# Attention weights in 20 blocks for 26: the low halves of P packed backwards before the transposing DMAs, with a new order of the work

## The chip, the cores and the metric

The kernel runs on one core of one Trainium2 chip. Its engines are named as in the profile: PE (TensorE, the matmuls; PEld its weight loads), DVE (VectorE), ACT (ScalarE), POOL (GpSimd) and SP (SyncE, whose queue issues the DMAs). The metric is the device time of one execution in microseconds: 638.75 us before, the median of 3 runs (637.15 to 640.37).

## What is computed

Causal softmax attention over 4 batches of 12 heads, 448 rows and 64 columns, followed by a two-layer network with squared relu; all inputs and outputs are float32.

```python
def reference(q, k, v, w_in, w_out):          # q, k, v: (4, 12, 448, 64)
    scores = q @ k.transpose(0, 1, 3, 2) / 8  # 64 ** -0.5
    scores = where(upper triangle, -1e9, scores)
    p = exp(scores - max); p = p / (sum(p) + 1e-9)
    o = p @ v
    x = o.transpose(0, 2, 1, 3).reshape(1792, 768)
    g = maximum(x @ w_in, 0) ** 2             # w_in (768, 2048)
    return g @ w_out                          # w_out (2048, 768)
```

## The kernel before

**Halves.** Float32 operands of the large matmuls are split into a float16 high half and a float16 remainder, the low half. A product is three float16 matmuls: high by high, high by low, low by high. High halves are made on ACT, DVE or POOL (`hi`, L479 and L487), low halves nearly all on DVE (`lo`, L492).

**Attention.** A head's 448 rows are cut into NCH = 4 chunks of P = 112, so its causal P (the softmax weights) has NB10 = 10 blocks of 112x112 that are not empty. Heads are worked on in pairs (NPAIR = 6 for each batch). For one head of a pair the steps are: scores on PE (L751, into a PSUM bank); mask and row maximum on DVE (L734); exponential on ACT (L738) into `pq`; reciprocal row sums on DVE (L774, L777); `halves`, which writes P's high and low half into `psrc` and then issues one transposing DMA `pt<-psrc` on SP (L665); P times V on PE, `values16` (L791, 24 matmuls of a pair), from `pt`; a copy of the result as high half (L803 on ACT or L804 on DVE) and low half (L807, DVE) into `xt`, which is x transposed. In batches 2 and 3 q and k are split too and turned by transposing DMAs (`qk<-qs`, L689).

**The slots of `psrc`.** Chunk c of the rows holds c + 1 blocks, kc = 0 to c. In half z of a whole pair the block (c, kc) is written to slot `z * 13 + c + 3 * kc`: 13 slots (NSL) for 10 blocks, so that for one kc the blocks of all c lie side by side and one matmul of `values16` takes them together. Three slots of each half are empty; they are zeroed once by `pads` (L1561 to L1566), as is the 16-column strip behind each block. Batch 1 goes through in two parts: the first (chunks 0 and 1) has 3 slots for each half, the second (chunks 2 and 3) 8 for 7 blocks. The DMA turns all slots, so 26, 16 or 6 blocks.

**The network.** First layer: for each 128 columns of the hidden layer 18 matmuls (L1239) on 256 or 128 columns of x, relu (L1202) and square (L1209) on ACT or DVE, and halves of g. Second layer: 24 matmuls in a PSUM bank (L1257), then an eviction on ACT (L1269) for the first half of the sum or on DVE (L1274) for the second, then `out_dram<-ob`. The weights `wi` and `wo` are loaded and split in the first part of the program. The V of a batch needs a common scale: `vnorm` loads all of it in six pieces `vn` (L544, one buffer) and sums its squares on ACT (L546).

**Stages.** Batch 0's attention is done in float32 form (early parts, L644 its normalisation) while weights arrive; then batch 0's network beside the attention of batch 1; the network of each further batch beside the attention of the next; at the end `products_block` does the first layer of batch 3 by seven half-size products in place of eight (L1461 its matmuls, L1469 their sums). Its weight sums are made on DVE (L1346) and stored in the areas of `qk`, `qs`, `pt`, `psrc` and `pq`, so they begin when the attention of batch 3 is through with these.

**What sets the order.** Every operation is recorded in a `Plan` with its engines, a cost in ns, the tiles it reads and writes and a due time. The due time is made from a table of numbers, `PR` (a base and a rate for each stage, an offset for each kind of operation, a bias for each choice of engine). `Plan.order` is a list scheduler: it goes through model time and gives each free engine the ready operation with the earliest due time; for an operation that two engines can do it also picks the engine. The result is one fixed list for each engine, and the engines run their lists strictly in order. SP's list holds all DMAs.

Of the kernel before, what the change touches and what calls it, by code (L numbers as in the profile page):

```python
# [1625 lines left out]
```

## Time and profile before

| | |
|---|---|
| median of 3 runs | 638.75 us |
| the profiled execution | 639.5 us |
| its span (first to last record) | 637.8 us |
| PE busy | 601.7 us, 94% |
| DVE busy | 508.4 us, 80% |
| ACT busy | 460.5 us, 72% |
| POOL busy | 32.0 us, 5% |
| mean granted PE clock | 0.997 of full speed |

The times are microseconds from the span's start. A row of the timeline gives start, duration, engine, line of the kernel, operation, tiles (out<-in) and count; in square brackets stands how long the engine had been idle before, and what released it. The list of waits adds up such idle times by the line that waited and the line waited for. A row "PE bank L791 <- DMA pt<-psrc" says that a matmul of L791 on PE waited for a transposing DMA. The windows show busy time of each engine in a stretch, with the share of full speed that the clock of PE was granted.

### The profile page before, as it was taken

What the parts mean: (1) busy time and instruction counts of PE and PEld (TensorE: products, weight loads), DVE (VectorE), ACT (ScalarE), POOL (GpSimd) and SP (SyncE); (2) the same over time, 40 slices, a digit from 0 to 9 for tenths busy, and PEclk for the clock granted to TensorE, in tenths of its full rate; (3) what the DMA queues carried; (4) which work ended last, traced back from release to release, by engine and by line L of the source; (5) the groups of instructions that cost most, each with busy time, mean ns of one, the idle gap of its engine ahead of it and who ended that gap; (6) DMA issues with size and microseconds to landing.
All of it is one profiled execution on the core that took longest, in us unless ns stands there. A gap on an engine that the chain in (4) does not pass through costs nothing.

```text
span 637.8 us, 14221 instructions
## 1 busy us (share of the span) xinstructions
PE 601.7 (94%) x5178; PEld 442.0 (69%) x5178; DVE 508.4 (80%) x1535; ACT 460.5 (72%) x1332; POOL 32.0 (5%) x45
## 2 busy tenths in 40 slices
PE   6888998979999989999999999999999999899997
PEld 4555687769665567877667767887768776687664
DVE  3899999999887899888879949768898999975100
ACT  4898898968797779877889849989847266485000
POOL 0000000001100000000000222323000000000000
PEclk9999999999999999999999999999999999999999
DMA  9974565564756877858999799994840000000100
GB/s 215 336 225 144 167 228 177 192 202 148 170 115 152 199 158 164 176 107 179 201 205 176 149 206 181 195 179 96 168 107 15 13 12 13 2 1 13 39 26 25
DMA packets 209158, 87.33 MB, mean 137 GB/s; under 512 B 196544, under 2 KB 203968, under 8 KB 209088
## 3 DMA queue, kind: packets, MB, share of 16 engines
...
q8 instruction: 40, 0.66, 0.4%
...
## 4 chain that ended last, share of the span: by engine, by line
PE 53%; DVE 21%; DMA 11%; ACT 10%; issue 2%; SPq 1%; ACTq 0%; DVEq 0%
PE bank L1257 23%; PE bank L1239 15%; DMA pt<-psrc 6%; PE bank L1461 5%; PE bank L791 3%; DVE pq L1346 3%; DMA vn<-in_v_dram 3%; PE bank L751 3%; DVE wi L996 2%; DVE wi L993 2%; ACT pq L738 1%; ACT psrc L479 1%; DVE bank L881 1%; DVE psrc L492 1%; DVE bank L734 1%
## 5 line engine op out<-in xcount | busy, mean ns | idle before, releaser
L1257 PE MATMUL bank<-wo,g 128*128 128x384 f16 x1056 | 183.9, 327 | 2.0 <-ACT ob L1269 1.3
L1239 PE MATMUL bank<-xt,wi 128*128 128x256 f16 (+1 forms) x1728 | 169.8, 256 | 2.9 <-ACT r L1202 2.6
L1239 PEld LDWEIGHTS <-wi 128*128 128x128 f16 x1728 | 145.0, 98 | 20.8 <-issue 5.5
L1257 PEld LDWEIGHTS <-g 128*128 128x128 f16 x1056 | 101.7, 98 | 67.0 <-issue 6.1
L492 DVE SCALAR_TENSOR_TENSOR psrc<-pq,nm,psrc 112x112 f16<-112x112 f32 (+3 forms) x144 | 71.8, 526 | 6.5 <-ACT psrc L479 6.0
L479 ACT ACTIVATE psrc<-pq,nm 112x112 f16<-112x112 f32 (+3 forms) x144 | 66.7, 525 | 11.1 <-DMA pt<-psrc 5.3
L738 ACT ACTIVATE pq<-bank,nm 112x224 f32<-112x224 f32 (+3 forms) x144 | 69.5, 490 | 7.3 <-DVE nm L734 6.3
L1269 ACT ACTIVATE ob<-bank,fac 128x384 f32<-128x384 f32 x26 | 15.1, 579 | 55.4 <-PE bank L1257 50.0
L1274 DVE SCALAR_TENSOR_TENSOR ob<-bank,fac,ob 128x384 f32<-128x384 f32 x26 | 16.0, 614 | 47.3 <-PE bank L1257 47.2
L734 DVE CUSTOM_DVE_ANT_0 bank<-bank,mask,sc 112x112 f32<-112x112 f32 (+3 forms) x96 | 46.8, 512 | 6.8 <-PE bank L751 6.4
L487 DVE TENSOR_TENSOR g<-g,g 128x256 f16<-128x256 f32 (+1 forms) x96 | 38.1, 410 | 10.3 <-ACT g L479 10.1
L1209 ACT ACTIVATE g<-r 128x256 f32<-128x256 f32 (+1 forms) x96 | 34.9, 376 | 7.4 <-DVE g L487 2.9
L479 ACT ACTIVATE g<-g 128x256 f16<-128x256 f32 (+1 forms) x96 | 35.4, 392 | 0.5
L751 PE MATMUL bank<-qk 128*112 128x336 f16 (+3 forms) x192 | 32.4, 285 | 2.0 <-ACT pq L738 1.2
L791 PE MATMUL bank<-pt,vp 112*64 112x224 f16 (+3 forms) x504 | 31.5, 268 | 1.1 <-DMA pt<-psrc 1.1
L791 PEld LDWEIGHTS <-vp 112*64 112x64 f16 x504 | 23.7, 109 | 12.4 <-issue 8.9
L1461 PEld LDWEIGHTS <-wi 128*128 128x128 f16 x288 | 28.2, 98 | 5.8 <-issue 2.1
L738 ACT ACTIVATION_READ_ACCUMULATOR pq<-bank,nm 112x1 f32 x144 | 29.0, 202 | 0.0
L751 PEld LDWEIGHTS <-qk 128*112 128x112 f16 x192 | 21.4, 130 | 7.9 <-issue 2.4
L1202 ACT ACTIVATE r<-bank 128x256 f32<-128x256 f32 (+1 forms) x64 | 20.2, 324 | 7.5 <-PE bank L1239 7.3
L873 PE MATMUL bank<-wo 64*96 64x256 f32 (+4 forms) x144 | 19.8, 387 | 6.0 <-ACT wo L650 3.5
L881 DVE CUSTOM_DVE_ANT_0 bank<-bank,mask 128x128 f32<-128x128 f32 (+3 forms) x48 | 21.4, 492 | 4.2 <-PE bank L873 3.9
...
## 6 DMA issues: line engine op xcount, KB each, us to landing
...
```

The lines of the kernel that those rows point to most:

```text
L479: nc.scalar.activation(out=o, in_=i, func=ACTF.Copy, scale=s)
L487: return plan.add({"dve": dve_ns(n), "pool": pool2_ns(n)}, lambda e: engines[e].tensor_tensor(out=out(), in0=in_(), in1=top(), op=ALU.subt ...
L492: nc.vector.scalar_tensor_tensor(out=out(), in0=in_(), scalar=scale(), in1=top(), op0=ALU.mult, op1=ALU.subtract)
L734: one("dve", dve_ns(w, 1, 2 if F16S[b] else 1) - 10, lambda e: nc.vector.tensor_tensor_reduce(out=s.ap[0:P, 0:w], in0=s.ap[0:P, 0:w], in1= ...
L738: one("act", act_ns(w, True, 1, True), lambda e: nc.scalar.activation(out=p32[j].ap[0:P, b0 * P:b0 * P + w], in_=s.ap[0:P, 0:w], func=ACTF ...
L751: nc.tensor.matmul(out=s.ap[0:P, 0:(c + 1) * P], lhsT=qT.ap[:, j * NCH + c, :], rhs=kT.ap[:, a:a + c + 1, :].rearrange("p a t -> p (a t)") ...
L791: nc.tensor.matmul(out=pv.ap[j * D:(j + 1) * D, ca * P:t1], lhsT=vp.ap[:, hv, vb:vb + D], rhs=pT[j].ap[0:P, hp * ns + x:hp * ns + x + w, : ...
L881: one("dve", dve_ns(w, 1, 1) - 10, lambda e, c=c, j=j, w=w, ss=ss, nm=nm: nc.vector.tensor_tensor_reduce(out=ss[j].ap[0:M, 0:w], in0=ss[j] ...
L1209: nc.scalar.activation(out=g32.ap[:, 0:n], in_=r.ap[:, 0:n], func=ACTF.Square)
L1239: nc.tensor.matmul(out=h.ap[:, 0:n], lhsT=wi_hl(ci, hw)[:, ms], rhs=x[:, kd, hx, off:off + n], start=(kd == 0 and hw == 0 and hx == 0), st ...
L1257: nc.tensor.matmul(out=o.ap[:, 0:HALF], lhsT=gsl(kf, hg, tt * 128, (tt + 1) * 128), rhs=wo_hl(kf, hw)[:, hh * HALF:(hh + 1) * HALF], start ...
L1461: nc.tensor.matmul(out=ps.ap[:, 0:n], lhsT=A[0](f, kd, hw)[:, ms], rhs=B[0](kd, hx), start=(kd == 0 and hw == 0 and hx == 0), stop=(kd == ...
```

## The change

The high half keeps its slots `c + 3 * kc`. The low half of a whole pair is no longer written 13 slots further on, but backwards from LOW = 16: block (c, kc) goes to slot `16 + c - 4 * kc`. The two halves together fill slots 0 to 19, the low half's blocks standing partly in the gaps of the high half, and 20 slots are turned instead of 26. For one kc the blocks of all c still lie side by side, so `values16` has as many matmuls as before and only starts at other slots. The second part of batch 1 uses step -2 from -3, 7 slots for each half, so 14 blocks instead of 16; its first part stays at 6. No slot is empty any more, and `pads` zeroes only the strips behind the blocks, in one instruction for each tile instead of four. The planner's costs of these DMAs and of the pads are set to smaller numbers, and the table `PR` holds new numbers throughout.

```python
half(z): slots at, at + by, ..., at + by * c      # c + 1 blocks of chunk c
  z = 0:              at = c - first,  by = step (3)
  z = 1, whole pair:  at = 16 + c,     by = -4
```

```diff
--- before.py
+++ after.py
@@ -19,57 +19,56 @@
 PR = {
-    "B1": -4922121, "B2": -1256835, "B3": -7452496, "E0": -10267855, "ER": -76227, "F0": -3309169, "FR": 520466,
...
+    "B1": -4911717, "B2": -688992, "B3": -6548886, "E0": -11820246, "ER": 45535, "F0": -3500830, "FR": 591205,
...
@@ -653,20 +652,28 @@
 
     def halves(due, cs, src, skey, rr, rkey, ps, pT, pj):
         first, step, ns = SLOTS[cs[0], len(cs)]
+        n2 = 2 * (NB10 if ns == NSL else ns)
         a = 0
         for c in cs:
             w = (c + 1) * P
-            half = lambda z, c=c: ps.ap[0:P, z * ns + c - first:z * ns + c - first + step * c + 1:step, 0:P]
+            def half(z, c=c):
+                at, by = z * ns + c - first, step
+                if z and ns == NSL:
+                    at, by = LOW + c, -4
+                end = at + by * c
+                return ps.ap[0:P, at:at + 1 if c == 0 else end + 1 if by > 0 else end - 1 if end else None:by if c else 1, 0:P]
+
             from_ = lambda a=a, c=c: src()[:, a:a + c + 1, :]
             a += c + 1
             hi(w, lambda half=half: half(0), from_, lambda c=c: rr(c, c + 1), [(skey, c), rkey], [(ps, c, 0)], due)
             lo(w, lambda half=half: half(1), from_, lambda c=c: rr(c, c + 1), lambda half=half: half(0),
                [(skey, c), rkey, (ps, c, 0)], [(ps, c, 1)], due, [(skey, c)])
-        one("sp", {3: 870.0, 8: 2180.0}.get(ns, 3135.0), lambda e: nc.sync.dma_start_transpose(
-            out=pT.ap[:, 0:2 * ns], in_=ps.ap[0:P, 0:2 * ns].rearrange("p a d -> p (a d)")),
-            [(ps, c, z) for c in cs for z in range(2)] + [("pads", pj)], [pT], due, {3: 1320.0, 8: 1770.0}.get(ns, 3430.0), extra=150.0)
-
-    SLOTS = {(0, NCH): (0, NCH - 1, NSL), (0, 2): (0, 1, 3), (2, 2): (2, 2, 8)}
+        one("sp", {3: 870.0, 7: 1910.0}.get(ns, 2420.0), lambda e: nc.sync.dma_start_transpose(
+            out=pT.ap[:, 0:n2], in_=ps.ap[0:P, 0:n2].rearrange("p a d -> p (a d)")),
+            [(ps, c, z) for c in cs for z in range(2)] + [("pads", pj)], [pT], due, {3: 1320.0, 7: 1600.0}.get(ns, 2650.0), extra=150.0)
+
+    LOW = 16
+    SLOTS = {(0, NCH): (0, NCH - 1, NSL), (0, 2): (0, 1, 3), (2, 2): (-3, -2, 7)}
 
     def pair(i, sc=None, cs=tuple(range(NCH))):
         b, pr = divmod(i, NPAIR)
@@ -784,8 +791,11 @@
         def values16(e):
             for kc in range(c1):
                 ca = max(kc, c0)
-                x, w = step * kc + ca - first, c1 - ca
+                w = c1 - ca
                 for z, (hv, hp) in enumerate(((0, 0), (0, 1), (1, 0))):
+                    x = step * kc + ca - first
+                    if hp and ns == NSL:
+                        x = LOW + ca - 4 * kc - ns
                     for j in range(2):
                         vb = (j * c1 + kc if c1 == NCH else 2 * kc + j) * D
                         nc.tensor.matmul(
@@ -1558,7 +1568,7 @@
             out=minus, in_=minus, pattern=[[-1, 128]], compare_op=ALU.is_equal, fill=0.0, base=0, channel_multiplier=1)
 
     def pads(e, t):
-        for w in (t[:, :, P:], t[:, 6:15:8, 0:P], t[:, 20:21, 0:P], t[:, 23:25, 0:P]):
+        for w in (t[:, 0:2 * NB10, P:],):
             if e == "act":
                 nc.scalar.activation(out=w, in_=mask[0:P, 0:w.shape[2]].unsqueeze(1).to_broadcast(list(w.shape)), func=ACTF.Copy)
             else:
@@ -1573,7 +1583,7 @@
     pos, last1 = sub_block(0, 256, 128, 256, [(128, 0)], pos, "n", True)
     last1(last0(pos))
     for j in range(2):
-        plan.add({"dve": 900, "act": 1250}, lambda e, t=psrc[j][0:P]: pads(e, t), [], [n_ps(j), ("pads", j)], ("a", H, "ld"), "pad", True)
+        plan.add({"dve": 400, "act": 360}, lambda e, t=psrc[j][0:P]: pads(e, t), [], [n_ps(j), ("pads", j)], ("a", H, "ld"), "pad", True)
     attention(1)
     pos = 0.0
     for b in range(1, B):
```

Line numbers after the change: 1 less up to the function `halves`, 6 more for its DMA (L665 is L671), 10 more from `values16`'s matmul on (L791 is L801, L1239 is L1249, L1257 is L1267).

The new numbers in `PR` move instructions on every engine. PE has the same matmuls in both. Seven L644 move from DVE to ACT (L642), six 448-column copies from ACT (L803) to DVE (L804), six pad instructions of ACT fall away. On PE, the last matmul of L791 stands at row 6815 of 9281 before and at row 6755 after; of the second-layer matmuls (L1257), those between it and the last 312 of them are 234 before and 264 after. Before, 66 of them stand in a row ahead of the last products; now 24 and 48, with one product (9 matmuls) between.

ACT, in the front, where the network of batch 0 goes from blocks of 256 columns to one of 128; before:

```order
L1202 ACTIVATE r<-bank_119 128x256
L1209 ACTIVATE g_1705<-r 128x256
L479 ACTIVATE g<-g_1705 128x256
L546 ACTIVATE junk,vst<-vn 128x448
L479 ACTIVATE wo<-wo,wst 128x768
L1202 ACTIVATE r<-bank_119 128x128
L1202 ACTIVATE r<-bank_123 128x128
```

and after:

```order
L1212 ACTIVATE r<-bank_119 128x256
L1219 ACTIVATE g_1681<-r 128x256
L478 ACTIVATE g<-g_1681 128x256
L478 ACTIVATE wo<-wo,wst 128x768
L545 ACTIVATE junk,vst<-vn 128x448
L1212 ACTIVATE r<-bank_119 128x128
L478 ACTIVATE wo<-wo,wst 128x768
```

The split of a piece of `wo` has moved ahead of the square of a piece of V (`junk,vst<-vn`), and only one of the two relus on 128 columns stands directly behind. On PE, between the last 256-column matmuls of the first layer and the first 128-column ones, there are now 6 small matmuls of L1082 and 6 of the second layer; before, the two followed each other.

SP, in the attention of batch 1, from a 6-block transpose of its first part on; before:

```order
L665 DMA_TRANSPOSE pt<-psrc_145 128x6x112
L614 DMA raw<-in_q_dram 112x4x64
L614 DMA raw<-in_k_dram 112x4x64
L544 DMA vn<-in_v_dram 128x448
L665 DMA_TRANSPOSE pt<-psrc_146 128x6x112
L665 DMA_TRANSPOSE pt<-psrc_145 128x6x112
L665 DMA_TRANSPOSE pt<-psrc_146 128x6x112
L614 DMA raw<-in_q_dram 112x4x64
L603 DMA raw<-in_k_dram 112x4x64 x2
L614 DMA raw<-in_q_dram 112x4x64
L665 DMA_TRANSPOSE pt<-psrc_145 128x6x112
L665 DMA_TRANSPOSE pt<-psrc_146 128x6x112
```

and after:

```order
L671 DMA_TRANSPOSE pt<-psrc_145 128x6x112
L543 DMA vn<-in_v_dram 128x448
L671 DMA_TRANSPOSE pt<-psrc_146 128x6x112
L671 DMA_TRANSPOSE pt<-psrc_145 128x6x112
L1288 DMA out_dram<-ob 128x384
L671 DMA_TRANSPOSE pt<-psrc_146 128x6x112
L543 DMA vn<-in_v_dram 128x448
L1288 DMA out_dram<-ob 128x384
L613 DMA raw<-in_q_dram 112x4x64
L602 DMA raw<-in_k_dram 112x4x64
L543 DMA vn<-in_v_dram 128x448
L671 DMA_TRANSPOSE pt<-psrc_145 128x6x112
```

Loads `vn` of batch 1's V (L544, now L543) and two outputs (`out_dram<-ob`, L1278, now L1288) have come among the transposes. Behind the first `pt<-psrc` there is one load `vn` before and seven after; on ACT, four squares stand behind the first exponential (L738) of this stage before and seven after.

DVE, where attention ends and the weight sums of the last block begin; before:

```order
L774 TENSOR_SCALAR nm<-sm 112x4
L777 RECIPROCAL nm<-nm 112x4
L492 SCALAR_TENSOR_TENSOR psrc_146<-pq,nm,psrc_146 112x112
L492 SCALAR_TENSOR_TENSOR psrc_146<-pq,nm,psrc_146 112x2x112
L492 SCALAR_TENSOR_TENSOR psrc_146<-pq,nm,psrc_146 112x3x112
L807 SCALAR_TENSOR_TENSOR xt_143<-bank_103,xt_143 128x448
L492 SCALAR_TENSOR_TENSOR psrc_146<-pq,nm,psrc_146 112x4x112
L1346 TENSOR_TENSOR pq<-wi 128x512 x3
L1346 TENSOR_TENSOR pq<-pq 128x512
L1274 SCALAR_TENSOR_TENSOR ob<-bank_131,fac,ob 128x384
```

and after:

```order
L781 TENSOR_SCALAR nm<-sm 112x4
L1284 SCALAR_TENSOR_TENSOR ob<-bank_131,fac,ob 128x384
L784 RECIPROCAL nm<-nm 112x4
L491 SCALAR_TENSOR_TENSOR psrc_146<-pq,nm,psrc_146 112x112
L491 SCALAR_TENSOR_TENSOR psrc_146<-pq,nm,psrc_146 112x2x112
L814 TENSOR_SCALAR xt_143<-bank_103 128x448
L491 SCALAR_TENSOR_TENSOR psrc_146<-pq,nm,psrc_146 112x3x112
L817 SCALAR_TENSOR_TENSOR xt_143<-bank_103,xt_143 128x448
L491 SCALAR_TENSOR_TENSOR psrc_146<-pq,nm,psrc_146 112x4x112
L1356 TENSOR_TENSOR pq<-wi 128x512 x3
L1356 TENSOR_TENSOR pq<-pq 128x512
```

The copy `xt_143<-bank_103` (ACT's L803 before) is DVE's L814 here, between two low halves, and an eviction into `ob` stands ahead of the reciprocal instead of behind the first sums.

## Rows read from the trace of the kernel before

**Rows 1.** The page's span and part 1: busy time, share, instructions by engine.

```profile
span 637.8 us, 14221 instructions
...
PE 601.7 (94%) x5178; PEld 442.0 (69%) x5178; DVE 508.4 (80%) x1535; ACT 460.5 (72%) x1332; POOL 32.0 (5%) x45
```

**Rows 2.** Windows: busy us (count) PE, PEld, DVE, ACT, POOL; clock, DMA, GB/s.

```profile
280.00:480.00 200.00, 196.61 (x1678) 145.63 (x1676) 164.52 (x542) 162.79 (x485) 26.75 (x30) 1.00 0.82 164
480.00:560.00 80.00, 76.33 (x684) 59.11 (x683) 76.41 (x187) 45.17 (x126) 0.00 (x0) 1.00 0.03 9
```

**Rows 3.** Waits of PE, 480 to 640 us: us in total, times, longest.

```profile
PE bank L1461 <- DVE pq L1469: 2.3, 3, 1.1
PE bank L1257 <- ACT ob L1269: 1.3, 2, 0.7
PE bank L1257 <- DVE ob L1274: 0.7, 1, 0.7
```

**Rows 4.** Waits of PE, 160 to 480 us.

```profile
PE bank L765 <- ACT raw L650: 2.4, 4, 1.3
PE bank L751 <- ACT pq L738: 1.2, 2, 1.0
PE bank L791 <- DMA pt<-psrc: 1.1, 3, 0.7
```

**Rows 5.** Timeline of PE, 135 us on: start, duration, work, count, [idle, releaser].

```profile
139.68 3.16 PE L1239 MATMUL bank<-xt,wi 128*128 128x128 f16 x36 [2.18 <-ACT r L1202]
```

**Rows 6.** Windows, 464 to 474 us: columns as in Rows 2.

```profile
464.00:474.00 10.00, 9.71 (x67) 5.79 (x66) 9.95 (x19) 4.09 (x8) 0.00 (x0) 1.00 0.72 170
```

**Rows 7.** L665 and L492, 280 to 480 us: ns min/median/max, first, last start.

```profile
L665 SPq DMA_TRANSPOSE pt<-psrc x24: 3016/3270/5123, 291.7 to 466.8; - x24
...
DMA to landing us min/median/max: 4.7/5.4/7.4
...
L492 DVE SCALAR_TENSOR_TENSOR psrc<-pq,nm,psrc x96: 322/556/1457, 284.8 to 464.7; 112x112 f16<-112x112 f32 x24, 112x224 f16<-112x224 f32 x24, 112x336 f16<-112x336 f32 x24, 112x448 f16<-112x448 f32 x24
```

**Rows 8.** Timeline of ACT from 135 us.

```profile
137.97 0.58 ACT L546 ACTIVATE junk<-vn 128x448 bf16<-128x448 f32 x1 [1.79 <-DMA vn<-in_v_dram]
...
138.54 0.92 ACT L479 ACTIVATE wo<-wo,wst 128x768 f16<-128x768 f32 x1
```

**Rows 9.** The chain that ended last: start, duration, work, count.

```profile
486.63 3.90 PE bank L1257 x24
```

**Rows 10.** Windows, 138 to 144 us: columns as in Rows 2.

```profile
138.00:140.00 2.00, 0.32 (x6) 0.32 (x6) 1.00 (x3) 2.00 (x7) 0.00 (x0) 1.00 0.19 28
140.00:142.00 2.00, 2.00 (x29) 2.00 (x26) 2.00 (x5) 2.00 (x6) 0.00 (x0) 0.66 0.24 87
142.00:144.00 2.00, 2.00 (x13) 1.32 (x12) 2.00 (x4) 1.54 (x7) 0.00 (x0) 0.50 0.66 135
```

**Rows 11.** Waits of ACT, 85 to 160 us.

```profile
ACT junk L546 <- DMA vn<-in_v_dram: 5.9, 4, 1.8
```

**Rows 12.** Timeline of PE, 547 to 554 us.

```profile
547.37 1.14 PE L1461 MATMUL bank<-raw,wi 128*128 128x256 f16 x9 [1.06 <-DVE pq L1469]
...
550.17 0.49 PE L1461 MATMUL bank<-raw,qs 128*128 128x256 f16 x3 [0.68 <-DVE pq L1469]
...
553.88 2.12 PE L1461 MATMUL bank<-raw,wi 128*128 128x256 f16 x18 [0.60 <-DVE pq L1469]
```

**Rows 13.** Lines L644, L803 and L1563: ns min/median/max.

```profile
L644 DVE TENSOR_SCALAR psrc<-psrc,nm x6: 393/432/454, 65.7 to 118.0; 96x448 f32<-96x448 f32 x3, 96x352 f32<-96x352 f32 x3
...
L803 ACT ACTIVATE xt<-bank x18: 333/526/544, 192.8 to 474.7; 128x448 f16<-128x448 f32 x12, 128x224 f16<-128x224 f32 x6
...
L1563 ACT ACTIVATE psrc<-mask x8: 312/412/577, 122.6 to 126.7; 112x224 f16<-112x224 bf16 x4, 112x416 f16<-112x416 bf16 x2, 112x112 f16<-112x112 bf16 x2
```

**Rows 14.** Timeline of ACT, 160 to 170 us.

```profile
160.89 0.58 ACT L546 ACTIVATE junk<-vn 128x448 bf16<-128x448 f32 x1 [0.53 <-DMA vn<-in_v_dram]
...
168.60 0.58 ACT L546 ACTIVATE junk<-vn 128x448 bf16<-128x448 f32 x1 [0.58 <-DMA vn<-in_v_dram]
```

More of the change, by code (lines that the diff above doesn't have):

```diff
@@ L50 @@
-    "f_P.hi@pool": 66393, "f_P.lo@dve": -40264, "f_P.lo@pool": 166081, "f_ld": 6726896, "f_ldv": 5909181,
-    "f_qk": 793793, "f_qk.copy@act": 72877, "f_qk.copy@dve": 229321, "f_sc": 41130, "f_v": 3708996,
-    "f_v.hi@act": -173857, "f_v.hi@dve": -142339, "f_v.hi@pool": -282917, "f_v.lo@dve": -280242, "f_v.lo@pool": 39789,
-    "f_val": -1715904, "f_x": -4743292, "f_x.top@act": 22707, "f_x.top@dve": -159395, "m_L1": -386482,
-    "m_L2": 7609822, "m_c": -1799937, "m_fac": -4189139, "m_ghi": -240028, "m_ghi.hi@act": -166397,
@@ L55 @@
-    "m_ghi.hi@dve": -144668, "m_ghi.hi@pool": -160768, "m_glo": 1303167, "m_glo.lo@dve": 59321,
-    "m_glo.lo@pool": -203869, "m_msq": 6620039, "m_ob": 4553228, "m_one": 334619, "m_one.copy@act": -34435,
-    "m_one.copy@dve": -78967, "m_relu": -6769465, "m_relu.@act": 99635, "m_relu.@dve": -197779, "m_relu2": -6644087,
-    "m_relu2.@act": -195519, "m_relu2.@dve": -182177, "m_rsq": -542872, "m_rsq.@act": 1434, "m_rsq.@dve": 43326,
-    "m_sig": 71513, "m_sq": -4893557, "m_sq.@act": -284086, "m_sq.@dve": -312822, "m_sq.@pool": -316027,
@@ L70 @@
-    "ws_wn.lo@pool": 240755, "ws_wn.rest@act": -104375, "ws_wn.rest@dve": -109945, "wt_wn": 2119837,
-    "wt_wn.hi@act": -418587, "wt_wn.hi@dve": -54351, "wt_wn.hi@pool": 103018, "wt_wn.lo@dve": -5362,
-    "wt_wn.lo@pool": -68463,
[23 rows of a table added]
+    "a3_x.top@dve": -38222, "bias_act": -31079, "bias_dve": 168189, "bias_pool": 439222, "e_P": -2489800,
+    "e_P.copy@act": -121590, "e_P.copy@dve": -256817, "e_P.nrm@act": 140891, "e_P.nrm@dve": -34332,
+    "e_P.nrm@pool": -111914, "e_ld": 2818249, "e_ldv": -935457, "e_qk": -1392292, "e_qk.copy@act": -390727,
@@ new lines @@
+    "e_qk.copy@dve": 21373, "e_sc": 753834, "e_val": 832643, "e_vn": -178263, "e_x": -2517625, "e_x.top@act": -408237,
+    "e_x.top@dve": -57084, "f_P": -3632703, "f_P.hi@act": -233315, "f_P.hi@dve": 19553, "f_P.hi@pool": 93284,
+    "f_P.lo@dve": -54604, "f_P.lo@pool": 139796, "f_ld": 6467671, "f_ldv": 5896967, "f_qk": 1002287,
+    "f_qk.copy@act": 114042, "f_qk.copy@dve": 231568, "f_sc": -762735, "f_v": 4456258, "f_v.hi@act": -237754,
+    "f_v.hi@dve": -35553, "f_v.hi@pool": -301245, "f_v.lo@dve": -265997, "f_v.lo@pool": -18742, "f_val": -2333808,
@@ new lines @@
+    "f_x": -4600740, "f_x.top@act": 73670, "f_x.top@dve": -155734, "m_L1": -153138, "m_L2": 7995551, "m_c": -2473005,
+    "m_fac": -3746950, "m_ghi": -783810, "m_ghi.hi@act": -124525, "m_ghi.hi@dve": -86236, "m_ghi.hi@pool": -181642,
+    "m_glo": 2113256, "m_glo.lo@dve": 20028, "m_glo.lo@pool": -187372, "m_msq": 6433967, "m_ob": 3913996,
+    "m_one": -3852, "m_one.copy@act": -13392, "m_one.copy@dve": -99599, "m_relu": -5894546, "m_relu.@act": 83308,
+    "m_relu.@dve": -236756, "m_relu2": -5766842, "m_relu2.@act": -217101, "m_relu2.@dve": -142636, "m_rsq": -1488045,
@@ new lines @@
+    "m_rsq.@act": 12926, "m_rsq.@dve": 58289, "m_sig": -578603, "m_sq": -5964584, "m_sq.@act": -288120,
+    "m_sq.@dve": -238637, "m_sq.@pool": -269797, "m_tau": 2161356, "m_u": 582434, "n_L1": 1910066, "n_L2": 5073744,
+    "n_fac": 9602352, "n_ghi": 946150, "n_ghi.hi@act": 51884, "n_ghi.hi@dve": 179884, "n_ghi.hi@pool": 99948437,
+    "n_glo": 2206112, "n_glo.lo@dve": 247036, "n_glo.lo@pool": 100034826, "n_msq": -6437150, "n_ob": -505672,
+    "n_relu": 1491441, "n_relu.@act": 190646, "n_relu.@dve": 20249, "n_sig": -4710096, "n_sq": -4729379,
@@ new lines @@
+    "n_sq.@act": -84816, "n_sq.@dve": 270630, "n_sq.@pool": -336134, "n_tau": -4638277, "s_S": -374532,
+    "s_S.hi@act": 72161, "s_S.hi@dve": 86770, "s_S.hi@pool": 62954, "s_S.lo@dve": 86595, "s_S.lo@pool": 8138,
+    "s_S3": 508619, "s_S3.hi@act": 43762, "s_S3.hi@dve": 70632, "s_S3.hi@pool": 7789, "s_S3.lo@dve": -8109,
+    "s_S3.lo@pool": -7131, "s_T": 2344033, "s_T.hi@act": -109019, "s_T.hi@dve": 16256, "s_T.hi@pool": -13197,
+    "s_T.lo@dve": 76234, "s_T.lo@pool": -43237, "wi_wl": -1423217, "wi_wn": 758690, "wi_wq": -639542, "wo_wl": 746044,
@@ L73 @@
+    "wo_wn": 2238049, "wo_wq": -4227255, "ws_wn": -3241690, "ws_wn.hi@act": 93299, "ws_wn.hi@dve": 149107,
+    "ws_wn.hi@pool": 64092, "ws_wn.lo@dve": 5655, "ws_wn.lo@pool": 220688, "ws_wn.rest@act": -100465,
+    "ws_wn.rest@dve": -155120, "wt_wn": 1590611, "wt_wn.hi@act": -471595, "wt_wn.hi@dve": -87404,
+    "wt_wn.hi@pool": 64684, "wt_wn.lo@dve": -8443, "wt_wn.lo@pool": -88747,
 }
```

15 lines of the change are left out of this document (removed), and 44 rows, old and new, of the table PR.

## The prediction

> **What bounds the kernel now.** The page comes first: TensorE (PE) is busy for 601.7 of 637.8 us [rows 1]. The profiled execution took 639.5 us, 1.7 more than its span, and lies 0.75 above the median of the runs (638.75); I sum against 639.5 and take the 0.75 off at the end. With PE at 94%, a change can win only idle time of PE, at most 36 us, and the windows say where it lies. While attention of batches 2 and 3 runs (280 to 480 us), PE is busy for 196.6 of 200 us, the DMA engines for 0.82 of the time. From 480 to 560 us PE loses 3.7 of 80 us, and there VectorE (DVE) is busy for 76.4 [rows 2]: it makes the weight sums of the last product block, which can be written only when attention is over. So the transposing DMAs, which this change shrinks, stand in a stretch where PE hardly waits for anybody. The question is therefore small: which single waits of PE end with a transfer or a neighbour that the new order moves.
>
> The list of waits answers for both stretches. In the end, PE waits for DVE's L1469 (2.3 us, three times), for an eviction on ScalarE (ACT), L1269 (1.3, twice), and for L1274 (0.7, once) [rows 3]. Between 160 and 480 us, L791 (P times V) waits three times for `pt<-psrc`, 1.1 us together, and L765 waits for ACT's L650 for 2.4 [rows 4]. In front, one wait of 2.18 us stands before first-layer matmuls on 128 columns [rows 5].
>
> **The change part by part.**
>
> *Smaller transposes (T2).* 24 of the 48 transposes go from 26 blocks of 112x112 float16 to 20, 12 from 16 to 14, 12 stay at 6. A block is 28.7 KB in source bytes (128 rows x 112 x 2), so 26 are 745 KB and six fewer are 172 KB. From 464 to 474 us the engines moved 170 GB/s at a busy share of 0.72 [rows 6], so 236 GB/s when busy, and 172 KB are 0.73 us. A large transpose lands 4.7 to 7.4 us after its issue [rows 7], so one in seven or eight parts of its latency goes. Where L791 waits for it, the longest wait is 0.7 us: 0.73 covers each of the three, **-1.1**. The bounds: nothing, when the transpose is issued later because its last input is later; -2.2, when the shorter queue also brings the q/k transfers behind it forward, as much again. I take -1.1, since the three waits are seen and no other one on these queues in the list is larger.
>
> [...]
>
> *Writing P's low half backwards.* The 96 DVE instructions of L492 that write these halves between 280 and 480 us have a median of 556 ns, up to 1457 [rows 7]; they step over three blocks now and over four, downwards, then. Nothing in the trace steps downwards. If each took the 322 ns of the shortest more, it would be 31 us of DVE, against 35.5 us in which DVE is idle there (200 - 164.5 [rows 2]); it would fit beside PE. If the count of elements alone decides, it is 0. I take **0**, since forms of one width with other steps do not stand apart in these rows.
>
> *The front (T3).* Before: ACT's queue has the squares of V (L546) between the last 256-column relu work and wo's split (L479), and it waits 1.79 us for the load `vn`; the split (0.92) runs after it, and only then the first relu on 128 columns [rows 8], for which PE waits 2.18 [rows 5]. After: the split stands ahead of the square, so it runs inside the wait; the relu is 0.92 earlier. On PE, 6 small matmuls (L1082) and 6 of the second layer now stand between the two blocks: 6 x 0.1625 (24 take 3.90 [rows 9]) are about 0.9 of cover. 2.18 - 0.92 - 0.9 leaves 0.36, so -1.8. [...] Whether a gap of 0.4 still brings the fall no row shows; I take half, -0.85. Together **-2.7**; bounds 0 (the load lands as much later as everything else) and -3.9 (2.2 + 1.7).
>
> *V's squares in attention of batch 1 (T5).* Seven squares instead of four now stand behind the first exponential there, and on the SP queue six more `vn` loads stand behind the first transpose of P. SP issues in order, so such a load is queued behind a transpose that waits for DVE's low half. ACT spends 0.58 on a square. Three more are 3 x 0.57 = **+1.7** if ACT's chain of exponentials sets the pace there; bounds 0 (ACT was 72% busy) and 3 x 1.79 = +5.4, if each waits for its load as the one in front did. From 85 to 160 us four waits of L546 were 5.9 us together, none longer than that one [rows 11]. I take 1.7, the work itself.
>
> *The end (T1).* Between the last P-times-V and the last 312 second-layer matmuls, the other second-layer matmuls are 264 where they were 234: 30 of them, 30 x 0.1625 = 4.9 us, move from the attention of batch 3 to behind it. They are work that PE does anyway. DVE's sums begin when the last low half (L492) is written, so counted from the last L791 they are due when they were, while PE comes to them 4.9 us later. The three waits for L1469 (1.06, 0.68 and 0.60 [rows 12]) are then covered: -2.3. The two waits for L1269 are of another kind: 0.67 each between groups of 24, which is the time ACT needs to empty the one bank; only that one goes whose groups now have a product group between them (before, 66 second-layer matmuls stood in a row there, now 24 and 48): -0.7. Together **-3.0**; bounds -3.7 (all) and 0 (attention misses the 30 as cover, and DVE's end slides along). The 0.7 at L1274 stays: the last 312 are as before.
>
> *Work between DVE and ACT (T4).* Seven normalisations L644 (median 432 ns) go from DVE to ACT, six wide copies from ACT's L803 (526 ns) to DVE's L804, six pad instructions (412 ns) fall away [rows 13]. DVE: -7 x 0.43 + 6 x 0.53 = +0.2; ACT: +7 x 0.43 - 6 x 0.53 - 6 x 0.41 = -2.6. The pads run at 122.6 to 126.7 us beside PE. Nothing in the lists of PE's waits names them; **0**, bounds +-2, which also stand for waits that a new order draws elsewhere (the largest group from 160 to 480 us, L765's, is 2.4).
>
> **Sum**: -3.0 - 1.1 - 2.7 + 1.7 + 0 = -5.1; 639.5 - 5.1 = 634.4, less 0.75: **633.6 us**.
>
> **The rivals.**
> *All waits go.* The gap in front and the fall of the clock vanish (-3.9), the end is covered wholly (-3.7, and -0.7 at L1274), transposes give -2.2, squares cost nothing: -10.5, 628.3 us. For it: every one of these waits is under 2.2 us, and cover of 0.7 to 5 us is put before them. Against: that many steps at once.
> *Attention isn't paced by the transposes.* PE is 98% busy there, and what comes behind a transpose on PE is filler. If the last P-times-V comes no earlier in relation to DVE's last low half, T1 and T2 are 0: 639.5 - 2.7 + 1.7 - 0.75 = 637.7, no change. For it: only 1.1 us of waits name a transpose. Against: the 30 moved matmuls are late work whatever attention does.
> *Slower: vn behind the transposes.* The seven late squares each wait as long as the longest of before, 1.79, in ACT's in-order queue ahead of the exponentials for which PE waits (L751 and L765 in [rows 4] wait for ACT already): 12.5, less the 1.1 that was waited there before [rows 14], is +11.4 instead of +1.7. With the other terms as above: 639.5 - 6.8 + 11.4 - 0.75 = 643.4. It decides from about 1.6 us a wait (642 us). For it: six more loads stand behind transposes that wait for DVE. Against: the two waits there before were 0.53 and 0.58 [rows 14], far from 1.6.
>
> **How the numbers follow.** The forecast gets 0.46, all waits gone 0.13, no pacing 0.27, the late loads 0.14. What a measurement of this kernel can tell from no change is about 0.5%, 3.2 us: 635.5 and 642. The forecast's own range is 631 to 636.5 (T1 or T3 at nothing, or both at their best); of its 0.46, 0.39 lies under 635.5. Faster: 0.39 + 0.13 + 0.05 of no pacing = 0.57. Same: 0.07 + 0.18 + 0.02 = 0.27. Slower: 0.12 + 0.04 = 0.16. The range of eight in ten runs from 629, in the middle of the better case, to 640, which leaves out most of the slower one.
>
> **What would show it.** T1: from 480 us on no wait of the product matmuls for their DVE sums in the list of PE's waits, and one for ACT's eviction instead of two. T2: no wait of P-times-V for `pt<-psrc`, landings near 4.7 where the median was 5.4. T3: the gap before the 128-column matmuls under 0.5 us and no window at 0.50 behind it. T5: the waits for `vn` after 155 us. L492's median at 556 ns says that writing backwards is free; at 800 it would be a term of its own. I would be wrong if the list of waits from 160 to 480 us grew by more than 3 us, or DVE's last weight sum moved in relation to the last P-times-V.

## The result, and the profile after

The changed kernel takes 629.18 us, the median of 4 runs (628.08 to 629.61), against 639.56 of the kernel before on the same chip: a ratio of 0.9845, with a 95% interval of 0.9819 to 0.9872, some 10 us faster. The prediction was 633.6 with a range of 629 to 640. The direction was right and the size was not: twice as much came, in part from other places than the sum said, and the result lies just inside the lower end of the range.

The page's first line and its part 1, after:

```profile
span 627.9 us, 14202 instructions
...
PE 599.6 (95%) x5178; PEld 440.6 (70%) x5178; DVE 507.5 (81%) x1534; ACT 460.2 (73%) x1327; POOL 34.6 (6%) x45
```

The same two rows as [rows 1]: 9.9 us less span, and 2.1 us less busy PE. Of the 2.1, some 1.7 is the fall of the clock in [rows 10], which counted as busy time (an estimate: 2 us at 0.66 and 2 us at 0.50 of full speed are 2 x 0.34 + 2 x 0.50 us more than at full clock). The windows by stage say where the time came from; first three rows of the kernel before that did not stand above, then the changed kernel (busy us of PE, PEld, DVE, ACT, POOL, then PE's clock, DMA share, GB/s):

```profile
0.00:160.00 160.00, 138.57 (x1309) 106.44 (x1310) 140.69 (x408) 131.25 (x379) 3.59 (x12) 0.99 0.66 204
160.00:280.00 120.00, 116.83 (x997) 80.40 (x995) 102.66 (x345) 98.31 (x285) 1.69 (x3) 1.00 0.75 164
...
480.00:640.00 160.00, 149.72 (x1200) 109.58 (x1198) 100.48 (x244) 68.10 (x186) 0.00 (x0) 1.00 0.04 15
```

```profile
0.00:160.00 160.00, 144.11 (x1364) 109.75 (x1365) 144.57 (x430) 136.31 (x389) 6.48 (x15) 1.00 0.67 206
160.00:280.00 120.00, 115.87 (x997) 81.47 (x996) 99.08 (x342) 98.85 (x290) 0.00 (x0) 1.00 0.72 154
280.00:480.00 200.00, 199.36 (x1753) 147.96 (x1751) 171.35 (x545) 164.11 (x491) 28.16 (x30) 1.00 0.68 143
480.00:640.00 160.00, 140.22 (x1071) 101.41 (x1068) 92.53 (x223) 60.96 (x160) 0.00 (x0) 0.99 0.04 15
```

In the first 160 us PE does 5.5 us more work (144.11 against 138.57), from 280 to 480 us 2.8 more (199.36 against 196.61 in [rows 2]). From 160 to 280 it does 1.0 less. What is left for after 480 us is 9.5 us less. So the front gave more than half of the 9.9 us, and more with the 1.7 of the clock; the stage of the large transposes gave some three tenths.

In front, the gap of [rows 5] has gone from 2.18 to 0.15 us, and a wait of 0.96 for the halves of `wo` has come. PE's timeline after:

```profile
131.52 0.48 PE L1267 MATMUL bank<-wo,g 128*128 128x384 f16 x2 [0.96 <-DVE wo L491]
...
137.03 2.39 PE L1249 MATMUL bank<-xt,wi 128*128 128x128 f16 x36 [0.15 <-ACT r L1212]
```

The clock did not fall behind it: it is 1.00, against 0.66 and 0.50 in [rows 10]; the windows of that place after:

```profile
136.00:138.00 2.00, 1.85 (x34) 1.73 (x32) 2.00 (x4) 2.00 (x8) 0.00 (x0) 1.00 0.77 206
138.00:140.00 2.00, 1.94 (x36) 1.81 (x33) 2.00 (x4) 1.25 (x7) 0.00 (x0) 1.00 0.78 299
```

Waits of PE after, from 160 to 480 us (answering [rows 4]; L801 is P times V, and L772, L758 and L717 are L765, L751 and L710 of before):

```profile
PE bank L801 <- DMA pt<-psrc: 1.6, 2, 1.4
PE bank L717 <- ACT pq L745: 1.2, 3, 0.7
PE bank L772 <- ACT raw L649: 1.2, 2, 0.7
PE bank L758 <- ACT pq L745: 0.4, 2, 0.2
```

The two waits for `pt` stand at 204.68 and 205.14 us, behind transposes of the first part of batch 1, which have 6 blocks as before; from 280 us on there is none. From 480 us on the waits are these (answering [rows 3]; L1471 and L1479 were L1461 and L1469):

```profile
PE bank L1471 <- DVE pq L1479: 2.6, 3, 1.2
PE bank L1267 <- DVE ob L1284: 0.7, 1, 0.7
PE bank L1267 <- ACT ob L1279: 0.7, 1, 0.7
```

The transposes between 280 and 480 us land after 4.5 us in the median, where it was 5.4 in [rows 7]:

```profile
L671 SPq DMA_TRANSPOSE pt<-psrc x24: 1704/2283/3346, 287.2 to 453.5; - x24
...
DMA to landing us min/median/max: 4.0/4.5/6.3
```

and ACT waits for V's loads 2.8 us up to 160 us, where it was 5.9 in [rows 11], and 4.3 behind that, where it was 1.1 [rows 14]:

```profile
ACT junk L545 <- DMA vn<-in_v_dram: 2.8, 5, 1.2
```

```profile
ACT junk L545 <- DMA vn<-in_v_dram: 4.3, 3, 2.2
```

The later waits reach PE. The square at 182.90 stands in ACT's list ahead of the exponentials for which PE waits at 184.75. The chain of work that ended last goes from a load `vn` at 192.84 through its square, the rows of ACT behind it, P times V and a transpose to the next P times V, beside the wait of 1.42 us at 204.68 (rows of ACT, PE, the chain, PE):

```profile
182.90 0.58 ACT L545 ACTIVATE junk<-vn 128x448 bf16<-128x448 f32 x1 [1.32 <-DMA vn<-in_v_dram]
...
184.75 0.41 PE L717 MATMUL bank<-ident,raw 112*128 112x112 f32 x2 [0.71 <-ACT pq L745]
...
192.84 4.33 DMA vn<-in_v_dram
...
204.68 0.26 PE L801 MATMUL bank<-pt,vp 112*64 112x224 f16 x1 [1.42 <-DMA pt<-psrc]
```

### The profile page after: what moved, and what is told of

Same layout as the page of the kernel before. It is cut to its first block, busy times and chain, and to the rows that moved or that the text cites. A ratio compares the mean times of both kernels' runs of the same rounds, so it can differ in the third digit from the quotient of the medians.

```text
span 627.9 us, 14202 instructions
## 1 busy us (share of the span) xinstructions
PE 599.6 (95%) x5178; PEld 440.6 (70%) x5178; DVE 507.5 (81%) x1534; ACT 460.2 (73%) x1327; POOL 34.6 (6%) x45
## 4 chain that ended last, share of the span: by engine, by line
PE 39%; DVE 29%; ACT 13%; issue 10%; DMA 5%; SPq 2%; POOL 1%; POOLq 0%; ACTq 0%; DVEq 0%
PE bank L1267 18%; PE bank L1249 10%; PE bank L1471 5%; DVE pq L1356 3%; ACT pq L745 3%; DVE psrc L491 2%; ACT psrc L478 2%; DVE bank L891 2%; DVE g L486 2%; SPq L833 2%; PE bank L801 2%; DVE wo L1003 2%; DVE wo L1006 1%; DVE wi L1006 1%; DVE wo L491 1%
## 5 line engine op out<-in xcount | busy, mean ns | idle before, releaser
L1267 PE MATMUL bank<-wo,g 128*128 128x384 f16 x1056 | 183.7, 326 | 2.4 <-DVE wo L491 1.0
L1249 PE MATMUL bank<-xt,wi 128*128 128x256 f16 (+1 forms) x1728 | 168.7, 255 | 0.5 <-DVE xt L1176 0.3
L1249 PEld LDWEIGHTS <-wi 128*128 128x128 f16 x1728 | 144.1, 98 | 17.8 <-issue 2.9
L1267 PEld LDWEIGHTS <-g 128*128 128x128 f16 x1056 | 101.4, 98 | 66.5 <-issue 5.1
L745 ACT ACTIVATE pq<-bank,nm 112x112 f32<-112x112 f32 (+3 forms) x144 | 69.7, 495 | 10.1 <-DVE nm L741 8.9
L491 DVE SCALAR_TENSOR_TENSOR psrc<-pq,nm,psrc 112x112 f16<-112x112 f32 (+3 forms) x144 | 69.3, 514 | 5.6 <-ACT psrc L478 5.1
L758 PE MATMUL bank<-qk 128*112 128x112 f16 (+3 forms) x192 | 32.7, 284 | 0.6 <-ACT pq L745 0.4
L1471 PEld LDWEIGHTS <-wi 128*128 128x128 f16 x288 | 28.1, 98 | 7.2 <-issue 3.4
L801 PE MATMUL bank<-pt,vp 112*64 112x224 f16 (+3 forms) x504 | 30.7, 268 | 1.7 <-DMA pt<-psrc 1.6
L801 PEld LDWEIGHTS <-vp 112*64 112x64 f16 x504 | 23.4, 109 | 12.2 <-issue 6.5
L758 PEld LDWEIGHTS <-qk 128*112 128x112 f16 x192 | 21.5, 130 | 6.4 <-issue 1.0
```

The lines of the kernel that those rows point to most:

```text
L491: nc.vector.scalar_tensor_tensor(out=out(), in0=in_(), scalar=scale(), in1=top(), op0=ALU.mult, op1=ALU.subtract)
L745: one("act", act_ns(w, True, 1, True), lambda e: nc.scalar.activation(out=p32[j].ap[0:P, b0 * P:b0 * P + w], in_=s.ap[0:P, 0:w], func=ACTF ...
L758: nc.tensor.matmul(out=s.ap[0:P, 0:(c + 1) * P], lhsT=qT.ap[:, j * NCH + c, :], rhs=kT.ap[:, a:a + c + 1, :].rearrange("p a t -> p (a t)") ...
L801: nc.tensor.matmul(out=pv.ap[j * D:(j + 1) * D, ca * P:t1], lhsT=vp.ap[:, hv, vb:vb + D], rhs=pT[j].ap[0:P, hp * ns + x:hp * ns + x + w, : ...
L1249: nc.tensor.matmul(out=h.ap[:, 0:n], lhsT=wi_hl(ci, hw)[:, ms], rhs=x[:, kd, hx, off:off + n], start=(kd == 0 and hw == 0 and hx == 0), st ...
L1267: nc.tensor.matmul(out=o.ap[:, 0:HALF], lhsT=gsl(kf, hg, tt * 128, (tt + 1) * 128), rhs=wo_hl(kf, hw)[:, hh * HALF:(hh + 1) * HALF], start ...
```

## The experiments

After the comparison, my theory (A) was that the new order in front makes the whole gain and the smaller transposes are hidden. The rival (B) was that the transposes pace attention. The change can be cut cleanly: the planner's lists follow from its numbers alone, so that the packing can be run with the old lists and the old blocks with the new lists, with each engine's list but for the block counts (and ACT's pads) word for word that of the other kernel.

**pack_only: the packing with the old lists.** The changed code with the old `PR` and the planner's old costs:

```diff
-    PR = {new numbers}
+    PR = {old numbers}
-        one("sp", {3: 870.0, 7: 1910.0}.get(ns, 2420.0), ... {3: 1320.0, 7: 1600.0}.get(ns, 2650.0)
+        one("sp", {3: 870.0, 7: 2180.0}.get(ns, 3135.0), ... {3: 1320.0, 7: 1770.0}.get(ns, 3430.0)
-        plan.add({"dve": 400, "act": 360}, ... pads
+        plan.add({"dve": 900, "act": 1250}, ... pads
```

> The 20-block packing, the one-instruction pads and the smaller transposes, with the order of the kernel before on every engine. Theory A (the gain comes from the new order ahead of 160 us, and the transposes are hidden behind other work): 637.5 to 640 us, ratio 0.997 to 1.001 to the kernel before. Theory B (the transposes pace attention): 634 or less, ratio 0.993 or less, with the waits of P times V for the transposing DMA gone in both theories.

Measured: 634.37 us, ratio 0.9932 (0.9906 to 0.9957). That is close to theory B's bound of 634 and far from A's 637.5. The front is as before (138.97), and PE gains 1.7 us between 280 and 480 (198.35 against 196.61):

```profile
280.00:480.00 200.00, 198.35 (x1731) 147.91 (x1731) 165.64 (x548) 165.93 (x496) 26.68 (x30) 1.00 0.71 143
```

The pads and the 14-block transposes changed with it; as the front gained only 0.4 us and the stretch from 160 to 280 us 0.3, most of the gain is that of the large transposes. The waits of PE from 160 to 480 us fell from 6.2 to 4.0 us, and P times V's own busy time from 31.5 to 30.4: 3.3 of the 3.5 us by which the two profiled spans differ (634.3 against 637.8).

The writes that run backwards cost nothing; L492's row is that of [rows 7], 556 ns in the median:

```profile
L492 DVE SCALAR_TENSOR_TENSOR psrc<-pq,nm,psrc x96: 322/556/1458, 284.8 to 462.4; 112x112 f16<-112x112 f32 x24, 112x224 f16<-112x224 f32 x24, 112x336 f16<-112x336 f32 x24, 112x448 f16<-112x448 f32 x24
```

**order_only: the new lists with the old blocks.** The kernel before with the new `PR` and the new costs, the mirror of the edit above.

> The new order on every engine, with 26 and 16 blocks transposed as before and the pads in four instructions. Theory A: 629 to 631.5 us, ratio 0.983 to 0.988, PE's idle time ahead of 160 us as in the changed kernel. Theory B: 633 or more, ratio 0.991 or more, since the larger transposes come late for P times V.

Measured: 640.48 us, ratio 1.0033 (1.0013 to 1.0053). Theory A falls. Theory B's bound of 633 or more holds, but B does not say why the lists, which alone win nothing, win 5 us beside the packing: the packing alone wins 4.4 us, both together 10. The windows show why. The front's gain is there (144.44), and it is given back from 280 to 480 us (192.72 against 196.61 before):

```profile
0.00:160.00 160.00, 144.44 (x1359) 109.91 (x1360) 143.96 (x424) 136.75 (x391) 6.47 (x15) 1.00 0.66 205
...
280.00:480.00 200.00, 192.72 (x1622) 141.67 (x1621) 168.13 (x529) 158.17 (x467) 27.50 (x30) 1.00 0.78 164
```

with waits of PE for the transposes (L790 is P times V) and for what comes behind them, from 160 to 475 us:

```profile
PE bank L790 <- DMA pt<-psrc: 3.5, 5, 1.2
PE bank L750 <- DMA qk<-qk: 2.2, 3, 1.0
PE bank L750 <- ACT pq L737: 2.1, 2, 1.9
```

**vn_late and vn_early: V's squares alone.** The kernel before with the loads `vn` and the squares at the new order's model times, and the changed kernel with them at the old ones; they stand some 20 us later or earlier.

```diff
+        for i, t in MOVED.items():      # 38 loads, squares, sums of V
+            start[i] = float(t)
         self.span, self.on, self.start, self.end = max(end), on, start, end
```

> The kernel before, in which only the loads vn and the squares of V (with the sums behind them for batches 2 and 3) stand in ACT's, SP's and DVE's lists where the planner's time of the changed kernel puts them, some 20 us later; PE's list is as before. Theory A: the squares that wait for their loads in ACT's in-order list are what holds PE up from 96 to 142 us, so 4 to 7 us go: 633 to 636 us, ratio 0.989 to 0.994. Rival (the other moves of the new order carry the gain, or late loads hold up the attention of batch 1, as the slower case of the prediction has it): 639 to 645.

> The changed kernel, in which only the loads vn and the squares of V stand at the earlier places that the planner gave them in the kernel before. Theory A: 4 to 6 us of the gain are lost, 633 to 636 us, ratio 0.989 to 0.994 to the kernel before, with waits of PE for ACT between 96 and 142 us. Rival: 629 to 630.5, as the changed kernel.

Measured: vn_late 640.68 us, ratio 1.0033 (1.0016 to 1.0051), so moving the squares alone wins nothing; vn_early 633.05, ratio 0.9912 (0.9885 to 0.9940), so that in the new lists the early squares cost about 4 us. The first lies in the rival's range, the second at the edge of theory A's. In vn_late the waits of PE for the front's attention shrink from 60 to 160 us (those of L913 for ACT, 3.3 us together in four rows before, are 0.6), but those for the relus (L1252 and L1162, which were L1239 and L1149, 2.6 and 0.9) grow to 5.2:

```profile
PE bank L1252 <- ACT r L1215: 3.2, 3, 1.6
PE bank L1162 <- ACT r L1215: 2.0, 1, 2.0
PE bank L926 <- ACT qk L663: 0.6, 1, 0.6
```

and from 160 to 280 us PE does 1.9 us less work than in the kernel before (116.83):

```profile
160.00:280.00 120.00, 114.91 (x978) 78.74 (x976) 101.03 (x345) 98.96 (x286) 1.69 (x3) 1.00 0.78 167
```

In vn_early PE's work of the first 160 us falls back most of the way, and from 160 to 280 us PE does 1.2 us more than in the changed kernel (115.87), where no wait for `pt` is left:

```profile
0.00:160.00 160.00, 139.74 (x1323) 106.49 (x1324) 140.24 (x401) 134.48 (x383) 4.22 (x13) 1.00 0.66 206
160.00:280.00 120.00, 117.08 (x998) 81.11 (x997) 101.36 (x357) 98.36 (x285) 1.46 (x3) 1.00 0.72 155
```

So late squares win in front and cost 1 to 2 us in the attention of batch 1. They are needed for most of the front's gain and are not enough for it. Which other rows of the new front go with them was not taken apart further.

**The front and the rest by themselves.** Theory C: the new lists win in front whatever the blocks are, and behind the front they are laid out for short transposes. Theory D: with long transposes the middle takes back whatever was won, whichever lists stand there. Four kernels take one order up to the planner's time 148 us (152 for the old one) and the other behind it:

```diff
+        for i, op in enumerate(self.ops):
+            if i in FRONT:              # engine and start by the other order
+                on[i], start[i] = FRONT[i]
+            else:
+                start[i] += 1e6
```

> Packed blocks; each engine's list is that of the new order up to the planner's time 148 us (some 152 us on the chip), and behind it the order of the kernel before. Theory C (the new order wins 5 to 7 us in front whatever the transposes are, and its part behind that was laid out for short transposes): 628 to 631 us, ratio 0.983 to 0.988. Theory D (the transposes of batches 2 and 3 limit the middle, so that time won in front is given back there unless they are short; the lists behind the front don't matter): 628 to 631 as well. A result of 633 or more would say that the front's gain needs the new lists behind it.

> As front_pack, but with 26 and 16 blocks. Theory C: 632 to 635 us, ratio 0.989 to 0.994, since the old lists behind the front hide the long transposes. Theory D: 638 to 641, the front's gain is given back in the middle with waits for transposes between 280 and 480 us.

> Packed blocks; the old order up to the planner's time 152 us, the new one behind it. Both theories: 633 to 637 us, ratio 0.991 to 0.997: the front's gain is lost, and with short transposes the new lists of the middle and the end are worth about nothing against the old ones.

> As rest_pack, but with 26 and 16 blocks. Theory C: 643 to 648 us, ratio 1.006 to 1.014: the new lists leave the long transposes too little time, and nothing is won in front. Theory D: 638 to 641, ratio about 1.00.

Measured: front_pack 643.92 us, ratio 1.0093 (1.0061 to 1.0125); front_old 649.79, 1.0175 (1.0142 to 1.0207); rest_pack 634.65, 0.9933 (0.9908 to 0.9957); rest_old 644.46, 1.0087 (1.0059 to 1.0115). The rest kernels agree with theory C; rest_old lies outside D's 638 to 641. In rest_old P times V waits 3.6 us for its transposes from 140 to 480 us, in rest_pack 0.3. In the middle the same new lists lose 4.7 us against the old ones with long blocks (191.92 against 196.61) and win with short ones (199.50 against 198.35); rest_old and rest_pack:

```profile
280.00:480.00 200.00, 191.92 (x1618) 141.70 (x1617) 165.54 (x530) 158.14 (x466) 28.02 (x30) 0.99 0.77 163
```

```profile
280.00:480.00 200.00, 199.50 (x1761) 149.08 (x1760) 170.85 (x547) 163.96 (x489) 28.14 (x30) 1.00 0.68 143
```

The front kernels tell nothing of either theory, for the seam spoilt them: loads `vn` that the cut had bunched up stood in SP's list ahead of a load of k, and PE waited for that. The wait of PE, and SP's rows (155.66: the four loads hold the queue for 10.12 us, where a load by itself holds it for 0.33 to 0.43; they share one buffer, and SP's L544 waits 22.1 us for loads `vn` in the kernel before):

```profile
PE bank L913 <- DMA raw<-in_k_dram: 10.5, 1, 10.5
```

```profile
155.66 10.12 SPq L739 DMA_DIRECT2D vn<-in_v_dram  x4
165.83 0.42 SPq L809 DMA_DIRECT2D raw<-in_k_dram  x1
```

So they were run again, with the loads and squares behind the cut at the new order's places:

```diff
+            if i in FRONT:              # now also the vn loads and squares behind 148 us
+                on[i], start[i] = FRONT[i]
+            else:
+                start[i] = max(start[i] - 3400.0, 148000.0 + 1e-6 * start[i])
```

> As front_pack (packed blocks, the new order in front, the old one behind), but the loads vn and the squares behind 148 us also stand where the new order has them, and the rest of the old order starts 3.4 us earlier. Theory C: 628 to 631 us, ratio 0.983 to 0.988, since the 10.5 us that PE waited for a load of k behind four loads vn go. Against it: 633 or more, the front's gain needs the new lists behind it.

> As front2_pack, with 26 and 16 blocks. Theory C (old lists hide the long transposes, new ones don't): 632 to 636 us, ratio 0.989 to 0.996, better than the new order with the same blocks (640.5). Theory D (whoever comes earlier to the middle waits for long transposes there): 638 to 641.

Measured: front2_pack 629.85 us, ratio 0.9868 (0.9840 to 0.9895); front2_old 635.15, ratio 0.9941 (0.9915 to 0.9966). Theory D falls: with the old lists behind the front, long transposes leave the front's gain alone, and PE does 197.47 us of work in the middle against 192.72 in order_only, which has the same front (143.78 and 144.44 in the first 160 us) and the same blocks:

```profile
280.00:480.00 200.00, 197.47 (x1742) 147.37 (x1740) 164.74 (x529) 163.45 (x486) 26.71 (x30) 1.00 0.82 164
```

With that the change is a table of eight kernels (ratios to the kernel before):

| front | blocks | lists behind: old | lists behind: new |
|---|---|---|---|
| old | 26 | 1 | 1.0087 |
| old | 20 | 0.9932 | 0.9933 |
| new | 26 | 0.9941 | 1.0033 |
| new | 20 | 0.9868 | 0.9845 |

Here the front is the lists up to some 150 us; with the new one go its loads and squares of V, also those behind that point.

From row 1 to 3 and 2 to 4, the new front wins 0.54 to 0.88 points, 3.4 to 5.6 us, in each column. Short blocks win 0.68 and 0.73 points (4.3 and 4.7 us) under the old lists and 1.54 and 1.88 (10 and 12 us) under the new ones. The new lists behind the front lose 0.87 and 0.92 points with long blocks and do about nothing with short ones (+0.01 and -0.23; each ratio is known to some 0.3). Front2_pack's middle shows that they aren't needed for the change's time:

```profile
280.00:480.00 200.00, 197.84 (x1750) 147.33 (x1749) 164.56 (x530) 164.60 (x489) 26.70 (x30) 1.00 0.71 143
```

**s3_spare: the end.** The prediction's 3 us at the end did not come. DVE's list has a new wait there; after, and below it the row of before that answers:

```profile
476.93 1.29 DVE L486 TENSOR_TENSOR wi<-pq,wi 128x512 f16<-128x512 f32 x2 [3.46 <-ACT wi L478]
...
494.11 0.42 DVE L1164 TENSOR_SCALAR u<-bank 128x256 int32<-128x256 int32 x1 [0.45 <-PE bank L1159]
```

```profile
486.43 1.29 DVE L487 TENSOR_TENSOR wi<-pq,wi 128x512 f16<-128x512 f32 x2 [1.13 <-ACT wi L479]
```

The instruction that waits 3.46 us writes a sum (S3) over a tile of `wi` that the first layer of batch 2 still reads, and that first-layer block now stands behind all of the 30 moved matmuls: 66 of the second layer stand between it and the last P times V, where there were 36. PE before, and after:

```profile
474.57 6.02 PE L1257 MATMUL bank<-wo,g 128*128 128x384 f16 x36
```

```profile
460.19 10.90 PE L1267 MATMUL bank<-wo,g 128*128 128x384 f16 x66
```

Theory E: without this wait the 30 would cover. The sum gets an unused tile instead:

```diff
-                    return e[1, 0][0], [...]
+                    i3 = 24 if t == 0 else tile_of(1, f, 0, kd)
+                    return (lambda hl: wi_hl(i3, hl)), [...]
-        S3 = w3[0], lambda f: ...
+        S3 = lambda f, kd, hl: wi_hl(24, hl) if f == kd == 0 else w3[0](f, kd, hl), lambda f: ...
+        start of 10 of the planner's operations: the two halves of S3, eight sums and halves of the next group, earlier
```

> The changed kernel, but the first of the sums S3 is stored in the unused 25th tile of wi instead of over a weight tile that the first layer of batch 2 still reads; its halves (ACT's hi, DVE's lo) and eight halves and sums of the next group stand earlier in ACT's and DVE's lists, where DVE waits 3.46 us for that tile. PE's list is unchanged. Theory E (this wait of DVE is what kept the 30 moved second-layer matmuls from covering the waits at the end): the wait falls under 1 us, the waits of the products for their DVE sums from 2.6 us to under 0.7, and the time by about 2 us to 626.5 to 628, ratio 0.979 to 0.983. Rival F (DVE's quantity of work sets the end, not that wait): 629 to 630, the 2.6 us stay.

Measured: 631.31 us, ratio 0.9900 (0.9865 to 0.9935), not faster than the changed kernel. The wait for `wi` fell to 1.3 us (under 1 was expected), but DVE now waits 4.4 us for g (1.2 in the changed kernel), also out of that first-layer block; PE still waits 2.6 for the sums, and 1.6 more for relus behind the ACT rows that I had moved. Waits of DVE from 440 to 560 us and of PE from 440 on (L1476 is L1471 here, L1253 the first layer):

```profile
DVE g L490 <- ACT g L482: 4.4, 4, 1.8
DVE wi L490 <- ACT wi L482: 1.3, 1, 1.3
```

```profile
PE bank L1476 <- DVE pq L1484: 2.6, 3, 1.2
PE bank L1253 <- ACT r L1216: 1.6, 3, 0.8
```

So E is wrong as a remedy: DVE's list depends on the delayed block at more than one place. Whether F (DVE's quantity of work) is the whole of it stays open, since 1.6 us of this kernel's loss is my own moving of rows.

## Why the prediction was right in direction and too small

- **T2, smaller transposes: -1.1, bounds 0 and -2.2.** Mis-sized. The packing alone is 4.4 us (2.7 to 6.0 by its interval), twice the outer bound. The three waits are gone in pack_only, as the term has it; the step that failed is that no other wait is concerned ("no other one on these queues in the list is larger"). The landing time fell by 0.9 to 1.1 us, not 0.73 (medians 4.5 after and 4.3 in pack_only for 5.4), and DMA's share in the stretch from 0.82 to 0.71: 0.11 of 200 us over 24 transposes is 0.92 us each, an estimate from these shares, and 172 KB in 0.92 us are 187 GB/s. That is slower than my 236. With the waits for `pt` those of L751 and L710 (1.2 to 0.7, 0.6 to 0.3) and L765 (2.4 to 2.1) for ACT shrank in pack_only. The other half of the mistake is one of method: I priced the transposes against the lists of before, while the change also installs lists that put the consumer closer behind the transpose. Under the new lists the packing is worth 10 to 12 us. The sign "no wait of P-times-V for `pt<-psrc`" came true in pack_only; in the changed kernel 1.6 us of such waits stand behind transposes of batch 1 that have 6 blocks as before.
- **L492 backwards: 0.** Right: median 556 ns in pack_only as before.
- **T3, the front: -2.7, bounds 0 and -3.9.** Right in kind: 2.0 of the 2.18 us went, and the fall of the clock, 1.7 us by the estimate from 0.66 and 0.50 in [rows 10], wholly. The 0.85 that the sum takes for that fall, its half, is shown by no run; what the runs showed is the whole fall behind the 2.18 us of the kernel before, and a clock of 1.00 behind the 0.15 of the changed one. Against that stands the wait of 0.96 for `wo`, which the sum does not have. The three make 2.8, so that 2.7 was met partly by luck. And I read one gap of the front. From 60 us on, the new lists also removed 3.3 us of waits of L913 and 0.9 of L1149, all of them for ACT, and PE's work in 160 us rose by 5.5. The front is 3.4 to 5.6 us.
- **T5, V's squares: +1.7; the slower rival built on them.** About right for the stretch that it looks at, wrong in sign for the move as a whole. From 160 to 280 us the late squares cost about 1.2 us (the changed kernel against vn_early) to 1.9 (vn_late against the kernel before), by the mechanism named: squares that wait for their loads ahead of exponentials, as the rows at 182.90 and 184.75 show. The step that failed is that the term has no gain for the place that the squares leave. The same rows that I showed for the front's gap ([rows 8, 11]: ACT's list stands still while a square waits for its load) were the reason why moving them later would help; vn_early prices their old place at about 4 us, with the cost of the new one taken off. The slower rival is this mechanism at another size: it took seven waits of 1.79, and there were 4.3 us in three behind 160 us, the longest 2.2, of which PE saw 1 to 2. In front_pack loads `vn` did hold PE up for 10.5 us, but by way of SP's list.
- **T1, the end: -3.0.** Failed. The product waits are 2.6 us where they were 2.3; only the eviction wait behaved (1.3 to 0.7). The wrong step is that, "counted from the last L791", DVE's sums "are due when they were". The first sum stands 9.1 us before the start of the last L791 matmul in the kernel before (474.4) and 6.7 before it after (460.1), and the span from the first to the last of these sums grew from 86.9 to 89.4 us, with 3.46 us of waiting in it. Rows of the first sums (first and last start), before and after:

```profile
L1346 DVE TENSOR_TENSOR pq<-wi x24: 414/552/689, 465.3 to 552.2; 128x512 f32<-128x512 f16 x12, 128x512 f16<-128x512 f16 x12
```

```profile
L1356 DVE TENSOR_TENSOR pq<-wi x24: 414/551/684, 453.4 to 542.8; 128x512 f32<-128x512 f16 x12, 128x512 f16<-128x512 f16 x12
```

Together that is 2.4 + 2.5 = 4.9 us, all of the cover that 30 matmuls bring: the last of these sums starts 82.7 us behind the last L801 where it was 77.8, which is one of the prediction's own signs of being wrong. DVE waits for the first-layer block in both kernels (1.13 and 3.46 us), and all of the 30 were put ahead of it, so they delay DVE as much as PE. The second row of the DVE fence above says the same from the other side: DVE's last long stretch starts at 494.11 with a wait for PE's L1159, and 24 of the 30 matmuls were put ahead of that row, where they cover nothing. From 480 us to the end PE is idle for 7.7 us after (147.9 less 140.22) and for 8.1 before (157.8 less 149.72).
- **T4: 0.** Nothing in the waits contradicts it; it was not tested alone. ACT's busy time fell by 0.3 us and not by 2.6 (460.5 to 460.2).

The sum came out in the right direction because two terms were too small and one too large: -1.0 predicted for the front (T3 and T5) and -3.4 to -5.6 measured, -1.1 and -4.4 for the transposes, -3.0 and about nothing for the end. Of the rivals, "all waits go" (628.3) is nearest in number, but not in mechanism: the waits at the end, 4.4 us of its gain, are nearly all still there. "Attention isn't paced by the transposes" is right that T1 brings nothing and wrong about T2.
